# Local attention scores in 64-key by 72-query tiles: one change to a four-layer transformer kernel on one core

## The chip, the cores and the metric

The kernel runs on one core of a Trainium2 chip. The metric is the device time of one execution in microseconds (us). Before the change it is 1339.9 us (median of 4 runs, 1339.5 to 1340.6).

## The reference, cut to what matters

Two attention layers alternate with two MLP layers over x of 2048 rows by 1024 columns (bf16). In attention each of 32 heads (32 wide) looks at 8 positions, two apart, its own and 7 earlier ones:

```python
W, dil = 8, 2
off = jnp.arange(W) * dil
idx = pos[:, None] - off[None, :]                 # query s sees s, s-2, ..., s-14
...
logits = jnp.einsum("bhsd,bhswd->bhsw", q, kg) * scale
attn = _softmax(jnp.where(mask, logits, -1e9), axis=-1)
o = jnp.einsum("bhsw,bhswd->bhsd", attn, vg)
return o.transpose(...).reshape(B, S, D) @ wo
```

The kernel sorts the rows by parity, so that "two apart" becomes "next to each other": a query then sees the 8 latest rows of its own parity, a band along the diagonal.

## The kernel before

Attention goes by *units*. A unit is 4 heads of 32 (together 128 rows of q and k) of one parity, 1024 positions; there are 8 x 2 = 16 units a layer. All SBUF and PSUM tiles come from pools that hand out a fixed number of buffers in turn; a scheduler orders the instructions of each engine by when they could run, so program order is only a priority.

```python
x2p = pool("x2p", 5)     # xr, xn, xs, xo: [128, 1024] bf16
rdp = pool("rdp", 2)     # reciprocals of the softmax sums: [128, 512] f32, the same 2 KB a row
psm = pool("psm", 2, PSUM); pss = pool("pss", 2, PSUM); psa = pool("psa", 1, PSUM)   # 2, 2 and 1 buffers of 2, 4 and 4 KB a row
...
def qk_chunk(u, wts, part, n):       # 512 columns of q (part 0) or k (part 1) for unit u
    for kt in range(KD):             # 8 matmuls 128x128 by 512
        nc.tensor.matmul(ps[:], lhsT=wts[part][...], rhs=hT[:, kt, lo:lo + 512], ...)
    dst = (qT, kT)[part][g % 2]
    nc.vector.tensor_copy(out=dst[:, lo:lo + 512], in_=ps[:])

def scores(u, r):                    # r = 0, 1, 2: 3, 3 and 2 tiles of 128 keys by 136 queries
    ss = [s_tile() for _ in range(2)]
    for t in ts:
        for h in range(HG):          # 4 heads = 4 row tiles of 32
            nc.tensor.matmul(ss[h // 2][:, h % 2, ...KW], lhsT=k[hp, lo:lo + P], rhs=q[hp, lo:lo + KW], ...)
    for b in range(2):
        nc.scalar.activation(out=pv, in_=ss[b][...], func=ACT.Exp, scale=scale, bias=shift[:])
        nc.vector.tensor_tensor(out=pv, in0=pv, in1=mk, op=ALU.mult)     # 0/1 band

def values(u, b, v, oT):             # half a unit: 4 key tiles
    ...                              # v and row sums in column tiles of 32, into acc (one buffer)
    rd = rdp.tile([P, 512], FP32, name="rd", tag="rd")
    nc.scalar.activation(out=rd[:], in_=acc[:, 1, :], func=ACT.Ln)
    nc.scalar.activation(out=rd[:], in_=rd[:], func=ACT.Exp, scale=-1.0)
    nc.vector.tensor_tensor(out=oT[g][...], in0=acc[:, 0, :], in1=rd[:], op=ALU.mult)

def out_proj(c, i, oT, wo, res, dst, h2):
    xr = x2("xr"); nc.sync.dma_start(out=xr[:], in_=res(c, i))           # residual rows
    xn = x2("xn")
    ...                              # 2 x 8 matmuls, each half: xn = ps + xr on VectorE
    nc.sync.dma_start(out=rows(dst, c, i), in_=xn[:])
...
for u in range(NU):                  # fill = the 4 q/k chunks of unit u+1; in the last unit 4 out_proj
    scores(u, 0); fill[0]()
    if u: values(u - 1, 1, v, oT)
    scores(u, 1); fill[1]()
    scores(u, 2); fill[2]()
    values(u, 0, v, oT); fill[3]()
```

The softmax here doesn't subtract the row's maximum and nothing guards it: scores larger than these inputs give would overflow.

Of the kernel before, what the change touches and what calls it, by code (L numbers as in the profile page):

```python
# [9 lines left out]
ACT = mybir.ActivationFunctionType  # L10
ALU = mybir.AluOpType
FP32 = mybir.dt.float32
BF16 = mybir.dt.bfloat16

P = 128
H = 32
DH = 32
W = 8
DIL = 2
# [6 lines left out]
def kernel(  # L26
# [15 lines left out]
    nc = tc.nc  # L42
# [4 lines left out]
    KD = D // P  # L47
    FT = F // P
    NT = S // P
    SC = S // DIL  # L50
    NI = SC // P
    NG = D // P
    HG = P // DH
# [4 lines left out]
    NW2 = 4  # L58
    HF = FT // NW2
    KW = P + W  # L60
    PAD = W
    SHIFT = 14.0
    assert D == H * DH and NT == 16 and NI == 8 and NG == 8 and HG == 4
    scale = float(DH) ** -0.5

    def pool(name, bufs, **kw):
        return ctx.enter_context(tc.tile_pool(name=name, bufs=bufs, **kw))

    const = pool("const", 1)
# [2 lines left out]
    vhp = pool("vhp", NT)  # L72
    gop = pool("gop", NFB)
    wp = pool("wp", 9)
    x2p = pool("x2p", 5)
    rdp = pool("rdp", 2)
    dram = pool("dram", 1, space=bass.MemoryType.DRAM)
    psm = pool("psm", 2, space=bass.MemoryType.PSUM)
    pss = pool("pss", 2, space=bass.MemoryType.PSUM)
# [20 lines left out]
    def x2(name, shape=None, dt=BF16):  # L100
        return x2p.tile(shape or [P, D], dt, name=name, tag="x2")
# [7 lines left out]
    def ln_exp_table():  # L109
# [10 lines left out]
    nc.vector.memset(shift[:], -SHIFT)  # L120
    ones = const.tile([P, DH], BF16, name="ones")
    nc.vector.memset(ones[:], 1.0)
    band = const.tile([P, KW], BF16, name="band")
    nc.gpsimd.memset(band[:], 1.0)
    nc.gpsimd.affine_select(out=band[:], in_=band[:], compare_op=ALU.is_ge, fill=0.0, base=0,
                            pattern=[[1, KW]], channel_multiplier=-1)
    nc.gpsimd.affine_select(out=band[:], in_=band[:], compare_op=ALU.is_ge, fill=0.0, base=W - 1,
                            pattern=[[-1, KW]], channel_multiplier=1)
    b1_bf = const.tile([P, FT], BF16, name="b1_bf")
    b2_bf = const.tile([P, NI, DIL], BF16, name="b2_bf")  # L130
    b1_sb = const.tile([P, FT], FP32, name="b1_sb")
# [12 lines left out]
    Pm = [pers.tile([P, HG, NI, KW], BF16, name=f"Pm{n}") for n in range(2)]  # L144
    for t in qT:
        nc.gpsimd.memset(t[:, S:S + PAD], 0.0)

    xa = [dram.tile([S, D], BF16, name=f"xa{li}") for li in range(2)]
    xb = dram.tile([S, D], BF16, name="xb")
# [29 lines left out]
    def norm_act(dst, x, mean, rs):  # L179
        bi = st("bi", [P, 1])  # L180
        nc.vector.tensor_scalar(out=bi[:], in0=mean, scalar1=rs[:], scalar2=-1.0, op0=ALU.mult, op1=ALU.mult)
        nc.scalar.activation(out=dst, in_=x, func=ACT.Identity, bias=bi[:], scale=rs[:])

    def cols(c, i):
        return slice((c * NI + i) * P, (c * NI + i + 1) * P)
# [34 lines left out]
    def load_qk(g2):  # L220
        ts = []
        for part in range(2):
            t = wt_("wqk", [P, KD, 256])
            nc.sync.dma_start(out=t[:], in_=wq_v[:, :, part * D + g2 * 256:part * D + (g2 + 1) * 256])
            ts.append(t)
        return ts

    def qk_chunk(u, wts, part, n):
        g, c = divmod(u, DIL)
        ps = m_tile()  # L230
        lo = c * SC + n * 512
        for kt in range(KD):
            nc.tensor.matmul(ps[:], lhsT=wts[part][:, kt, (g % 2) * P:(g % 2 + 1) * P], rhs=hT[:, kt, lo:lo + 512],  # L233
                             start=(kt == 0), stop=(kt == KD - 1))
        dst = (qT, kT)[part][g % 2]
        nc.vector.tensor_copy(out=dst[:, lo:lo + 512], in_=ps[:])  # L236

    def scores(u, r):
        g, c = divmod(u, DIL)
        q, k, pm = qT[g % 2], kT[g % 2], Pm[u % 2]  # L240
        ts = range(3 * r, min(3 * r + 3, NI))
        n = len(ts)
        ss = [s_tile() for _ in range(2)]
        for t in ts:
            lo = c * SC + t * P
            for h in range(HG):
                hp = slice(h * DH, (h + 1) * DH)
                nc.tensor.matmul(ss[h // 2][:, h % 2, (t - ts[0]) * KW:(t - ts[0] + 1) * KW],  # L248
                                 lhsT=k[hp, lo:lo + P], rhs=q[hp, lo:lo + KW], start=True, stop=True)
        for b in range(2):  # L250
            pv = pm[:, 2 * b:2 * b + 2, ts[0]:ts[0] + n, :]
            nc.scalar.activation(out=pv.rearrange("p h t k -> p h (t k)"), in_=ss[b][:, :, 0:n * KW], func=ACT.Exp,  # L252
                                 scale=scale, bias=shift[:])
            mk = band[:].unsqueeze(1).unsqueeze(1).to_broadcast([P, 2, n, KW])
            nc.vector.tensor_tensor(out=pv, in0=pv, in1=mk, op=ALU.mult)  # L255

    def values(u, b, v, oT):
        g, c = divmod(u, DIL)
        pm = Pm[u % 2]
        acc = a_tile()  # L260
        hb = NI // 2
        t0 = b * hb
        for i in range(-1 if b else 0, hb):
            t = t0 + i
            for h in range(HG):
                hp = slice(h * DH, (h + 1) * DH)
                lhs = v[c][t][:, g * P + h * DH:g * P + (h + 1) * DH]
                if i < 0:
                    nc.tensor.matmul(acc[hp, 0, 0:W], lhsT=lhs, rhs=pm[:, h, t, P:KW], start=True, stop=False,
                                     skip_group_check=True)  # L270
                else:
                    w = KW if i < hb - 1 else P
                    nc.tensor.matmul(acc[hp, 0, i * P:i * P + w], lhsT=lhs, rhs=pm[:, h, t, 0:w],  # L273
                                     start=(t == 0), stop=(i == hb - 1), skip_group_check=True)
        for h in range(HG):
            hp = slice(h * DH, (h + 1) * DH)
            nc.tensor.matmul(acc[hp, 1, :].rearrange("p (t q) -> p t q", q=P), lhsT=ones[:], rhs=pm[:, h, t0:t0 + hb, 0:P],  # L277
                             start=True, stop=False, skip_group_check=True)
        s0 = t0 - 1 if b else 0
        ns = t0 + hb - 1 - s0  # L280
        o0 = (s0 + 1 - t0) * P
        for h in range(HG):
            hp = slice(h * DH, (h + 1) * DH)
            dst = acc[hp, 1, :].rearrange("p (t q) -> p t q", q=P)[:, o0 // P:o0 // P + ns, 0:W]
            nc.tensor.matmul(dst, lhsT=ones[:], rhs=pm[:, h, s0:s0 + ns, P:KW], start=False, stop=True,  # L285
                             skip_group_check=True)
        rd = rdp.tile([P, 512], FP32, name="rd", tag="rd")
        nc.scalar.activation(out=rd[:], in_=acc[:, 1, :], func=ACT.Ln)  # L288
        nc.scalar.activation(out=rd[:], in_=rd[:], func=ACT.Exp, scale=-1.0)  # L289
        lo = c * SC + t0 * P  # L290
        nc.vector.tensor_tensor(out=oT[g][:, lo:lo + hb * P], in0=acc[:, 0, :], in1=rd[:], op=ALU.mult)  # L291

    def load_wo():
        tiles = []
# [8 lines left out]
    def out_proj(c, i, oT, wo, res, dst, h2):  # L303
        xr = x2("xr")
        nc.sync.dma_start(out=xr[:], in_=res(c, i))
        xn = x2("xn")
        for n in range(NDC):
            ps = m_tile()
            xs_ = slice(n * 512, (n + 1) * 512)
            for g in range(NG):  # L310
                nc.tensor.matmul(ps[:], lhsT=oT[g][:, cols(c, i)], rhs=wo[n][g // 4][:, g % 4, :],  # L311
                                 start=(g == 0), stop=(g == NG - 1))
            nc.vector.tensor_tensor(out=xn[:, xs_], in0=ps[:], in1=xr[:, xs_], op=ALU.add)
        nc.sync.dma_start(out=rows(dst, c, i), in_=xn[:])
        h2[c][i] = vhp.tile([P, D], BF16, name="h2", tag="vh")
        mean, rs = stats(xn, 1.0 + EPS, eps2)
        norm_act(h2[c][i][:], xn[:], mean, rs)

    order = [(c, i) for c in range(DIL) for i in range(NI)]

# [70 lines left out]
    NU = NG * DIL  # L391
    for li in range(2):
# [35 lines left out]
        oT = [gop.tile([P, S], BF16, name="oT", tag="go") for _ in range(NG)]  # L428
        h2 = [[None] * NI for _ in range(DIL)]
        chunks = [(0, 0), (1, 0), (0, 1), (1, 1)]  # L430
        for part, n in chunks:
            qk_chunk(0, wts, part, n)
        wo = None
        for u in range(NU):
            last = u == NU - 1
            if not last:
                if (u + 1) % (2 * DIL) == 0:
                    wts = load_qk((u + 1) // (2 * DIL))
                fill = [lambda part=part, n=n: qk_chunk(u + 1, wts, part, n) for part, n in chunks]
            else:  # L440
                fill = [lambda i=i: out_proj(0, i, oT, wo, res, xa[li], h2) for i in range(4)]
            if u == NU - 2:
                wo = load_wo()
            scores(u, 0)
            fill[0]()
            if u:
                values(u - 1, 1, v, oT)
            scores(u, 1)
            fill[1]()
            scores(u, 2)  # L450
            fill[2]()
            values(u, 0, v, oT)
            fill[3]()
        values(NU - 1, 1, v, oT)
        for c, i in order[4:]:
            out_proj(c, i, oT, wo, res, xa[li], h2)
        g = [None] * NFB
# [38 lines left out]
```

## Time and profile before

A line of a group reads: source line, engine, operation, output<-inputs, shapes, count | busy us, mean ns of one | idle time of the engine ahead of them, and what ended it. In the chain of waits each line is start, length and what the kernel was waiting for at that time, followed back from the last instruction; "issue" is time in which an engine waited for nothing that the profile shows. PEld are TensorE's weight loads, SPq and DVEq the queues of the sync engine and of VectorE. First, from the page of the kernel before: busy times, the chain by engine, and the exponentials and masks.

```profile
PE 1312.7 (98%) x8352; PEld 590.5 (44%) x8352; DVE 428.3 (32%) x774; ACT 406.7 (30%) x622; POOL 3.9 (0%) x13
...
PE 92%; ACT 6%; DMA 1%; issue 0%; DVE 0%; SPq 0%
...
L252 ACT ACTIVATE Pm<-s,shift 128x816 bf16<-128x816 f32 (+1 forms) x192 | 152.0, 859 | 39.6 <-PE s L248 39.6
L255 DVE TENSOR_TENSOR Pm<-Pm,band 128x816 bf16<-128x816 bf16 (+1 forms) x192 | 99.9, 532 | 29.5 <-ACT Pm L252 25.0
```

TensorE (PE) bounds the kernel. Most of the rest of the chain, 6% on ScalarE (ACT), sits in the attention stages. This is the chain of waits of the kernel before over one unit:

```profile
149.11 1.83 PE m L233 x8
150.94 0.29 PE s L248 x12
151.24 1.83 PE m L233 x8
...
153.44 0.22 PE acc L277 x4
153.66 0.06 PE acc L285 x4
153.72 0.02 issue
153.74 0.61 ACT rd L288
154.35 0.02 issue
154.37 0.63 ACT rd L289
155.00 1.67 ACT Pm L252 x2
156.67 0.04 issue
156.71 0.29 PE s L248 x4
157.00 1.62 PE m L233 x7
```

A unit takes 10.09 us (149.11 to 159.20). From 153.7 to 156.7 the chain leaves TensorE: the third score block waits for a free score tile, which two exponentials hold, which stand behind Ln and Exp of the values in ScalarE's queue.

Next, busy time of the engines in stretches of the kernel before (start:end, length, then busy us and count of PE, PEld, DVE, ACT and POOL, and last the granted clock, the DMA share and GB/s): one unit; 15 units of the first layer, from its first score to its first output projection; and from there to its last output projection.

```profile
149.11:159.20 10.09, 9.79 (x117) 4.29 (x118) 6.91 (x13) 7.09 (x10) 0.00 (x0) 1.00 0.35 106
81.49:231.86 150.37, 146.22 (x1725) 64.00 (x1725) 103.07 (x180) 105.37 (x148) 0.00 (x0) 1.00 0.09 25
231.86:289.64 57.78, 57.78 (x363) 26.03 (x356) 51.26 (x102) 33.05 (x57) 0.00 (x0) 1.00 0.47 150
```

In the unit VectorE (DVE, third) is busy 6.91 and ScalarE 7.09 of 10.09 us.

### The profile page before, as it was taken

The page shows a single profiled execution, that of the slowest core. Times are in us where ns is not written, and L with a number is a line of the kernel's source. Part 1 is how long each engine was busy: PE and PEld are TensorE (multiplying, and loading weights), DVE is VectorE, ACT ScalarE, POOL GpSimd, SP SyncE. Part 2 cuts the span into 40 slices and gives each one's busy share as a digit, 9 for nine tenths or more (in the row PEclk, how much of TensorE's full clock was granted, in tenths as well). Part 3 has the DMA queues.
Part 4 walks back from the last instruction along what each step waited for, and adds up shares of the span by engine and source line. Part 5 has one row for each costly group of instructions (what it writes and reads, how often), then busy time and mean ns, then how long its engine had stood idle before and what let it go on. Part 6 is the DMA issues. An engine that isn't in the chain of part 4 may idle for free.

```text
span 1338.2 us, 19150 instructions
## 1 busy us (share of the span) xinstructions
PE 1312.7 (98%) x8352; PEld 590.5 (44%) x8352; DVE 428.3 (32%) x774; ACT 406.7 (30%) x622; POOL 3.9 (0%) x13
## 2 busy tenths in 40 slices
PE   6999999999999999999999999999999999999998
PEld 2444444444444444444444444444444444444443
DVE  6246666960000013233210667678300000011111
ACT  4346766542111110000023677675311111000000
POOL 1000000000000000000000000000000000000000
PEclk8999999999999999999999999999999999999999
DMA  9521110462222226546431101124522221334420
GB/s 251 119 64 33 33 33 28 142 194 79 63 79 77 63 71 164 129 128 181 118 95 48 34 17 33 32 74 154 151 79 79 71 81 56 119 94 124 131 89 32
DMA packets 192195, 121.83 MB, mean 91 GB/s; under 512 B 34416, under 2 KB 173680, under 8 KB 192112
## 3 DMA queue, kind: packets, MB, share of 16 engines
q1 hardware_dynamic: 192000, 120.61, 32.0%
q8 instruction: 65, 1.06, 0.3%
q0 software_dynamic: 112, 0.01, 0.1%
q14 instruction: 18, 0.15, 0.0%
HBM read 96.48 MB, written 16.78 MB: 85 GB/s over the span
## 4 chain that ended last, share of the span: by engine, by line
PE 92%; ACT 6%; DMA 1%; issue 0%; DVE 0%; SPq 0%
PE s L337 14%; PE s L380 14%; PE m L233 13%; PE m L311 8%; PE m L216 8%; PE m L380 7%; PE m L337 7%; PE acc L337 7%; PE acc L380 7%; ACT Pm L252 3%; PE s L248 1%; PE acc L273 1%; ACT rd L289 1%; ACT rd L288 1%; PE acc L277 1%; DMA x<-in_A_x_dram 1%
## 5 line engine op out<-in xcount | busy, mean ns | idle before, releaser
L380 PEld LDWEIGHTS <-w 128*128 128x128 bf16 x1792 | 175.3, 98 | 211.4
L337 PEld LDWEIGHTS <-w 128*128 128x128 bf16 x1792 | 175.3, 98 | 211.4
L233 PE MATMUL m<-hT,wqk 128*128 128x512 bf16 x1024 | 247.0, 381 | 0.0
L337 PE MATMUL s<-h,w 128*128 128x512 bf16 x896 | 202.8, 379 | 0.0
L380 PE MATMUL s<-g,w 128*128 128x512 bf16 x896 | 199.9, 379 | 0.0
L383 DVE SCALAR_TENSOR_TENSOR xo<-s,b_sb,xs 128x512 bf16<-128x512 f32 x32 | 24.0, 751 | 540.7 <-PE s L380 536.5
L252 ACT ACTIVATE Pm<-s,shift 128x816 bf16<-128x816 f32 (+1 forms) x192 | 152.0, 859 | 39.6 <-PE s L248 39.6
L233 PEld LDWEIGHTS <-wqk 128*128 128x128 bf16 x1024 | 90.3, 98 | 109.2 <-issue 6.6
L216 PE MATMUL m<-wv,hT 128*128 128x512 bf16 x512 | 113.6, 384 | 4.8 <-ACT hT L199 3.7
L311 PE MATMUL m<-wo,oT 128*128 128x512 bf16 x512 | 112.2, 379 | 0.0
L255 DVE TENSOR_TENSOR Pm<-Pm,band 128x816 bf16<-128x816 bf16 (+1 forms) x192 | 99.9, 532 | 29.5 <-ACT Pm L252 25.0
L337 PE MATMUL acc<-h,w 128*128 128x512 bf16 x448 | 103.9, 379 | 0.0
L380 PE MATMUL acc<-g,w 128*128 128x512 bf16 x448 | 100.6, 379 | 0.0
L380 PE MATMUL m<-g,w 128*128 128x512 bf16 x448 | 99.3, 379 | 0.0
L337 PE MATMUL m<-h,w 128*128 128x512 bf16 x448 | 99.0, 379 | 0.0
L163 ACT ACTIVATE ln<-mv,eps 128x1 f32<-128x1 f32 x64 | 18.7, 293 | 236.9 <-DVE mv L171 236.7
L344 ACT ACTIVATE g<-s,b_sb 128x1024 bf16<-128x1024 f32 x28 | 31.2, 1113 | 166.9 <-PE s L337 166.9
L216 PEld LDWEIGHTS <-hT 128*128 128x128 bf16 x512 | 50.3, 99 | 66.8 <-ACT hT L199 4.4
L236 DVE CAST qT<-m 128x512 bf16<-128x512 f32 x64 | 44.0, 688 | 100.3 <-PE m L233 100.1
L311 PEld LDWEIGHTS <-oT 128*128 128x128 bf16 x512 | 49.3, 98 | 59.6 <-issue 0.9
L291 DVE TENSOR_TENSOR oT<-acc,rd 128x512 bf16<-128x512 f32 x64 | 44.2, 691 | 59.0 <-ACT rd L289 58.9
L288 ACT ACTIVATE rd<-acc 128x512 f32<-128x512 f32 x64 | 38.2, 596 | 66.7 <-PE acc L285 66.7
(50 smaller groups left out, 585.6 us busy)
## 6 DMA issues: line engine op xcount, KB each, us to landing
w<-in_B_w_dram SPq DMA_DIRECT2D x56, 512.0 KB, 3.8
w<-in_B_w_dram SPq DMA_DIRECT2D x64, 448.0 KB, 4.4
wqk<-in_A_wqkv_dram SPq DMA_DIRECT2D x16, 512.0 KB, 5.1
xa<-xn SPq DMA_DIRECT2D x32, 256.0 KB, 2.1
xs<-xa SPq DMA_DIRECT2D x32, 256.0 KB, 3.1
x<-in_A_x_dram SPq DMA_DIRECT2D x16, 256.0 KB, 6.6
wv<-in_A_wqkv_dram SPq DMA_DIRECT2D x8, 512.0 KB, 5.9
xr<-in_A_x_dram SPq DMA_DIRECT2D x16, 256.0 KB, 3.0
```

The lines of the kernel that those rows point to most:

```text
L216: nc.tensor.matmul(ps[:], lhsT=hT[:, kt, cols(c, i)], rhs=wv[n][kt // 4][:, kt % 4, :], start=(kt == 0), stop=(kt == KD - 1))
L233: nc.tensor.matmul(ps[:], lhsT=wts[part][:, kt, (g % 2) * P:(g % 2 + 1) * P], rhs=hT[:, kt, lo:lo + 512], start=(kt == 0), stop=(kt == KD ...
L236: nc.vector.tensor_copy(out=dst[:, lo:lo + 512], in_=ps[:])
L252: nc.scalar.activation(out=pv.rearrange("p h t k -> p h (t k)"), in_=ss[b][:, :, 0:n * KW], func=ACT.Exp, scale=scale, bias=shift[:])
L255: nc.vector.tensor_tensor(out=pv, in0=pv, in1=mk, op=ALU.mult)
L288: nc.scalar.activation(out=rd[:], in_=acc[:, 1, :], func=ACT.Ln)
L291: nc.vector.tensor_tensor(out=oT[g][:, lo:lo + hb * P], in0=acc[:, 0, :], in1=rd[:], op=ALU.mult)
L311: nc.tensor.matmul(ps[:], lhsT=oT[g][:, cols(c, i)], rhs=wo[n][g // 4][:, g % 4, :], start=(g == 0), stop=(g == NG - 1))
L337: nc.tensor.matmul(pairs[fl][0][dc], lhsT=wt[c][:, i, fl * P:(fl + 1) * P], rhs=h2[c][i][:, dc * 512:(dc + 1) * 512], start=(k == 0), stop ...
L344: nc.scalar.activation(out=g[fb][:, fl, :].rearrange("p (n d) -> p n d", n=2), in_=t[:], func=ACT.Gelu_apprx_tanh, bias=b1_sb[:, ft:ft + 1])
L380: nc.tensor.matmul(aps[dc], lhsT=w2t[ft // HF][:, ft % HF, c::DIL], rhs=g[ft // GF][:, ft % GF, dc * 512:(dc + 1) * 512], start=(ft == 0), ...
L383: nc.vector.scalar_tensor_tensor(out=xo[:, dc * 512:(dc + 1) * 512], in0=aps[dc], scalar=b2_sb[:, i, c:c + 1], in1=xs[:, dc * 512:(dc + 1) ...
```

## The change

Per unit only an 8-wide band of each 128 x 136 score tile is used. The change computes scores in tiles of 64 keys by 72 queries, so that half a unit's scores fit in the two score tiles. A unit becomes two *visits*, each with one block of scores, one of values and two projection chunks. The exponential runs on the compact form; the mask multiply writes it into dense tiles whose other parts stay zero. With it came: k is copied out of PSUM by ScalarE, the rd tiles move into the pool of xr and xn (to make room for the compact tiles), the output weights are asked for earlier, and the TensorE order is fixed.

```diff
-    x2p = pool("x2p", 5)
-    rdp = pool("rdp", 2)
+    x2p = pool("x2p", 6)
+    pcp = pool("pcp", 2)
...
         dst = (qT, kT)[part][g % 2]
-        nc.vector.tensor_copy(out=dst[:, lo:lo + 512], in_=ps[:])
+        if part:
+            nc.scalar.copy(out=dst[:, lo:lo + 512], in_=ps[:])
+        else:
+            nc.vector.tensor_copy(out=dst[:, lo:lo + 512], in_=ps[:])
...
+        for i in range(HB):
+            for r in range(2):
+                lo = c * SC + (b * HB + i) * P + r * HK
+                for h in range(HG):
+                    mm = nc.tensor.matmul(ss[h // 2][r * HK:(r + 1) * HK, h % 2, i * HW:(i + 1) * HW],
+                                          lhsT=k[hp, lo:lo + HK], rhs=q[hp, lo:lo + HW], start=True, stop=True)
+        pc = pcp.tile([P, HG, HB, HW], BF16, name="pc", tag="pc")
+        for n in range(2):
+            nc.scalar.activation(out=pc[:, 2 * n:2 * n + 2]..., in_=ss[n][:, :, 0:HB * HW], func=ACT.Exp, ...)
+        for r in range(2):
+            nc.vector.tensor_tensor(out=pm[rp, :, b * HB:(b + 1) * HB, r * HK:r * HK + HW], in0=pc[rp], in1=mk, op=ALU.mult)
...
-        rd = rdp.tile([P, 512], FP32, name="rd", tag="rd")
+        rd = x2("rd", [P, 512], FP32)
...
+    def in_order(f, *args):
+        with tc.issue_after(last_pe[0].ins) if last_pe[0] is not None else nullcontext():
+            last_pe[0] = f(*args)
...
+        for vis in range(2 * NU):
+            u, b = divmod(vis, 2)
+            ...
+            if vis == 2 * NU - 6:
+                wo = load_wo()
+            in_order(scores, u, b)
+            if vis:
+                in_order(values, *divmod(vis - 1, 2), v, oT)
+            for n in range(2):
+                if u + 1 < NU:
+                    in_order(qk_chunk, u + 1, wts, *chunks[2 * b + n])
+                else:
+                    in_order(out_proj, 0, 2 * b + n, oT, wo, res, xa[li], h2)
```

More of the change, by code (lines that the diff above doesn't have):

```diff
@@ L60 @@
     KW = P + W
+    HK = P // 2
+    HW = HK + W
     PAD = W
@@ L122 @@
     nc.vector.memset(ones[:], 1.0)
-    band = const.tile([P, KW], BF16, name="band")
+    band = const.tile([P, HW], BF16, name="band")
     nc.gpsimd.memset(band[:], 1.0)
-    nc.gpsimd.affine_select(out=band[:], in_=band[:], compare_op=ALU.is_ge, fill=0.0, base=0,
-                            pattern=[[1, KW]], channel_multiplier=-1)
-    nc.gpsimd.affine_select(out=band[:], in_=band[:], compare_op=ALU.is_ge, fill=0.0, base=W - 1,
-                            pattern=[[-1, KW]], channel_multiplier=1)
+    for r in range(2):
+        hb_ = band[r * HK:(r + 1) * HK]
+        nc.gpsimd.affine_select(out=hb_, in_=hb_, compare_op=ALU.is_ge, fill=0.0, base=0,
+                                pattern=[[1, HW]], channel_multiplier=-1)
+        nc.gpsimd.affine_select(out=hb_, in_=hb_, compare_op=ALU.is_ge, fill=0.0, base=W - 1,
+                                pattern=[[-1, HW]], channel_multiplier=1)
     b1_bf = const.tile([P, FT], BF16, name="b1_bf")
@@ L146 @@
         nc.gpsimd.memset(t[:, S:S + PAD], 0.0)
+    for t in Pm:
+        nc.gpsimd.memset(t[0:HK, :, :, HW:KW], 0.0)
+        nc.gpsimd.memset(t[HK:P, :, :, 0:HK], 0.0)
     xa = [dram.tile([S, D], BF16, name=f"xa{li}") for li in range(2)]
@@ L232, in qk_chunk @@
         for kt in range(KD):
-            nc.tensor.matmul(ps[:], lhsT=wts[part][:, kt, (g % 2) * P:(g % 2 + 1) * P], rhs=hT[:, kt, lo:lo + 512],
-                             start=(kt == 0), stop=(kt == KD - 1))
+            mm = nc.tensor.matmul(ps[:], lhsT=wts[part][:, kt, (g % 2) * P:(g % 2 + 1) * P], rhs=hT[:, kt, lo:lo + 512],
+                                  start=(kt == 0), stop=(kt == KD - 1))
         dst = (qT, kT)[part][g % 2]
-        nc.vector.tensor_copy(out=dst[:, lo:lo + 512], in_=ps[:])
@@ L238, in scores @@
-    def scores(u, r):
+        if part:
+            nc.scalar.copy(out=dst[:, lo:lo + 512], in_=ps[:])
+        else:
+            nc.vector.tensor_copy(out=dst[:, lo:lo + 512], in_=ps[:])
+        return mm
+    last_pe = [None]
+    def in_order(f, *args):
+        with tc.issue_after(last_pe[0].ins) if last_pe[0] is not None else nullcontext():
+            last_pe[0] = f(*args)
+    HB = NI // 2
+    def scores(u, b):
         g, c = divmod(u, DIL)
         q, k, pm = qT[g % 2], kT[g % 2], Pm[u % 2]
-        ts = range(3 * r, min(3 * r + 3, NI))
-        n = len(ts)
@@ L243, in scores @@
         ss = [s_tile() for _ in range(2)]
-        for t in ts:
-            lo = c * SC + t * P
-            for h in range(HG):
-                hp = slice(h * DH, (h + 1) * DH)
-                nc.tensor.matmul(ss[h // 2][:, h % 2, (t - ts[0]) * KW:(t - ts[0] + 1) * KW],
-                                 lhsT=k[hp, lo:lo + P], rhs=q[hp, lo:lo + KW], start=True, stop=True)
-        for b in range(2):
-            pv = pm[:, 2 * b:2 * b + 2, ts[0]:ts[0] + n, :]
-            nc.scalar.activation(out=pv.rearrange("p h t k -> p h (t k)"), in_=ss[b][:, :, 0:n * KW], func=ACT.Exp,
-                                 scale=scale, bias=shift[:])
-            mk = band[:].unsqueeze(1).unsqueeze(1).to_broadcast([P, 2, n, KW])
-            nc.vector.tensor_tensor(out=pv, in0=pv, in1=mk, op=ALU.mult)
+        for i in range(HB):
+            for r in range(2):
+                lo = c * SC + (b * HB + i) * P + r * HK
+                for h in range(HG):
+                    hp = slice(h * DH, (h + 1) * DH)
+                    mm = nc.tensor.matmul(ss[h // 2][r * HK:(r + 1) * HK, h % 2, i * HW:(i + 1) * HW],
+                                          lhsT=k[hp, lo:lo + HK], rhs=q[hp, lo:lo + HW], start=True, stop=True)
@@ new lines, in scores @@
+        pc = pcp.tile([P, HG, HB, HW], BF16, name="pc", tag="pc")
+        for n in range(2):
+            nc.scalar.activation(out=pc[:, 2 * n:2 * n + 2].rearrange("p h t k -> p h (t k)"), in_=ss[n][:, :, 0:HB * HW],
+                                 func=ACT.Exp, scale=scale, bias=shift[:])
+        for r in range(2):
+            rp = slice(r * HK, (r + 1) * HK)
+            mk = band[rp].unsqueeze(1).unsqueeze(1).to_broadcast([HK, HG, HB, HW])
+            nc.vector.tensor_tensor(out=pm[rp, :, b * HB:(b + 1) * HB, r * HK:r * HK + HW], in0=pc[rp], in1=mk, op=ALU.mult)
@@ L257, in values @@
+        return mm
     def values(u, b, v, oT):
@@ L284, in values @@
             dst = acc[hp, 1, :].rearrange("p (t q) -> p t q", q=P)[:, o0 // P:o0 // P + ns, 0:W]
-            nc.tensor.matmul(dst, lhsT=ones[:], rhs=pm[:, h, s0:s0 + ns, P:KW], start=False, stop=True,
-                             skip_group_check=True)
-        rd = rdp.tile([P, 512], FP32, name="rd", tag="rd")
+            mm = nc.tensor.matmul(dst, lhsT=ones[:], rhs=pm[:, h, s0:s0 + ns, P:KW], start=False, stop=True,
+                                  skip_group_check=True)
+        rd = x2("rd", [P, 512], FP32)
         nc.scalar.activation(out=rd[:], in_=acc[:, 1, :], func=ACT.Ln)
@@ L291, in values @@
         nc.vector.tensor_tensor(out=oT[g][:, lo:lo + hb * P], in0=acc[:, 0, :], in1=rd[:], op=ALU.mult)
+        return mm
     def load_wo():
@@ L310, in out_proj @@
             for g in range(NG):
-                nc.tensor.matmul(ps[:], lhsT=oT[g][:, cols(c, i)], rhs=wo[n][g // 4][:, g % 4, :],
-                                 start=(g == 0), stop=(g == NG - 1))
+                mm = nc.tensor.matmul(ps[:], lhsT=oT[g][:, cols(c, i)], rhs=wo[n][g // 4][:, g % 4, :],
+                                      start=(g == 0), stop=(g == NG - 1))
             nc.vector.tensor_tensor(out=xn[:, xs_], in0=ps[:], in1=xr[:, xs_], op=ALU.add)
@@ L317, in out_proj @@
         norm_act(h2[c][i][:], xn[:], mean, rs)
+        return mm
     order = [(c, i) for c in range(DIL) for i in range(NI)]
@@ L430 @@
         chunks = [(0, 0), (1, 0), (0, 1), (1, 1)]
+        last_pe[0] = None
         for part, n in chunks:
-            qk_chunk(0, wts, part, n)
+            in_order(qk_chunk, 0, wts, part, n)
         wo = None
-        for u in range(NU):
-            last = u == NU - 1
-            if not last:
-                if (u + 1) % (2 * DIL) == 0:
-                    wts = load_qk((u + 1) // (2 * DIL))
-                fill = [lambda part=part, n=n: qk_chunk(u + 1, wts, part, n) for part, n in chunks]
-            else:
-                fill = [lambda i=i: out_proj(0, i, oT, wo, res, xa[li], h2) for i in range(4)]
-            if u == NU - 2:
-                wo = load_wo()
-            scores(u, 0)
-            fill[0]()
-            if u:
-                values(u - 1, 1, v, oT)
-            scores(u, 1)
-            fill[1]()
-            scores(u, 2)
-            fill[2]()
-            values(u, 0, v, oT)
-            fill[3]()
-        values(NU - 1, 1, v, oT)
+        for vis in range(2 * NU):
+            u, b = divmod(vis, 2)
+            if b == 0 and u + 1 < NU and (u + 1) % (2 * DIL) == 0:
+                wts = load_qk((u + 1) // (2 * DIL))
+            if vis == 2 * NU - 6:
+                wo = load_wo()
+            in_order(scores, u, b)
[6 more added lines that the diff above has]
+                    in_order(out_proj, 0, 2 * b + n, oT, wo, res, xa[li], h2)
+        in_order(values, NU - 1, 1, v, oT)
         for c, i in order[4:]:
```

## The prediction

> **What bounds the kernel now.** TensorE: the page has PE busy 98% of the span, and the chain that ended last is 92% PE, 6% ACT. Only the attention stages change (81.5 to 248 and 739 to 906 us). There the chain of waits repeats every 10.09 us, once per unit (16 units a layer). From single TensorE starts in the unit at 149.1 us:
> - 32 projection matmuls at 216 ns: 6.91 us.
> - Scores, 32 matmuls: four row tiles start 3 to 4 ns apart, a round of four takes 54 to 60 ns: 0.45 us.
> - Values and sums, two blocks: 1.0 us.
> - 11 changes of tile form, about 95 ns each (the next start comes 310 ns after a projection matmul instead of 216): 1.05 us. The Trainium skill, "TensorEngine Tiling (Array Packing)", Key Properties, says that changing the tiling mode drains TensorE; this trace agrees.
> - The last scores sub-block waits for a score tile, behind exponentials and Ln/Exp (the chain goes through ACT rd, rd, Pm, Pm there): its starts come 0.15 and 0.30 us late, in four half-filled rounds (0.11 more): 0.55 us.
>
> ACT is busy 7.1 and DVE 6.9 us of the 10.09 (stretch view); neither bounds, but ACT's order makes that wait.
>
> **What the change does, per unit.**
> - Scores: 64 matmuls of N=72 on 8 tiles. At the start spacing seen, eight take some 30 ns if weight loads hide: I estimate 0.15 to 0.25 us per visit, 0.4 per unit, as before.
> - Form changes: scores, values, projections, twice: 6 instead of 11. Saves 0.5 us.
> - Exponentials: 4 of 576 columns instead of 4 of 816 and 2 of 544. From 0.93 and 0.715 us I estimate 0.74 each: 3.0 instead of 5.15 us. ACT gains two k copies (0.58 each, as for v): net -1.0.
> - Masks: 4 of 1152 columns; from 0.58 and 0.435 us I estimate 0.76 each: 3.05 instead of 3.2. DVE loses two k casts (1.36): net -1.5. Both engines are off the critical path.
> - Score tiles are reused once per visit (4.5 us) and the exponentials end about 2 us into it: the 0.55 us goes. New near-collision: the last scores round of a new unit needs the second q cast, which comes behind masks and oT in DVE's queue; I allow 0.1 us.
>
> New unit: 6.91 + 0.4 + 1.0 + 0.55 + 0.1 = about 9.0 us. Saving 1.1 us on 14 middle units and 1 us together on first and last, twice: about 33 us, all on the critical path. MLP and v stages should not move.
>
> **Prediction:** 1308 us (2.4% faster), 8 in 10 between 1297 and 1325. Faster by over 2%: 0.62; within 2%: 0.36; slower: 0.02.
>
> **What would show each step.** Visit period 4.4 to 4.6 us; scores block at most 0.25 us from first to last start; three form changes per visit at 85 to 100 ns; no ACT Pm or rd in the chain of middle units; exponentials 0.70 to 0.78 us, masks 0.70 to 0.82; ACT near 6.5 and DVE near 5.8 us per unit; gemm stages unchanged.
>
> **What would make it wrong.** Weight loads of 64 columns not hiding behind 72-column matmuls, or 60 short matmuls in a row arriving too slowly: scores of 0.45 us or more per visit would halve the gain (about 1320). Masks falling out of their fast rate (over 1.1 us each) would delay the q cast and stall each new unit by up to 1 us.

## More of the kernel before

Last, from the timeline of the kernel before (start, length, engine, line, what, count, and in brackets the idle time before it): the first residual load, and the four output projections in the last unit.

```profile
46.33 1.68 SPq L305 DMA_DIRECT2D xr<-in_A_x_dram  x1
...
231.86 3.63 PE L311 MATMUL m<-wo,oT 128*128 128x512 bf16 x16
...
236.32 3.63 PE L311 MATMUL m<-wo,oT 128*128 128x512 bf16 x16
...
240.11 3.63 PE L311 MATMUL m<-wo,oT 128*128 128x512 bf16 x16
...
244.24 3.63 PE L311 MATMUL m<-wo,oT 128*128 128x512 bf16 x16
```

The residual rows of the first output projection are loaded 186 us early, and none of these projections shows a wait in brackets.

## The result, and the profile after

The changed kernel takes 1325.4 us (median of 4, 1323.7 to 1326.3), against 1339.9. The ratio is 0.989, interval 0.9873 to 0.9907. It is 14.5 us faster where 32 were forecast, and just above the range's end of 1325. The change is clear of the noise but within 2%, to which the prediction gave 0.36.

The same lines of the page of the changed kernel:

```profile
PE 1280.5 (97%) x9220; PEld 590.7 (45%) x9376; DVE 388.0 (29%) x646; ACT 372.3 (28%) x622; POOL 11.6 (1%) x19
...
PE 85%; DVE 7%; ACT 4%; DMA 2%; issue 2%; SPq 0%; DVEq 0%; ACTq 0%
...
L275 DVE TENSOR_TENSOR Pm<-pc,band 64x1152 bf16<-64x1152 bf16 x128 | 96.4, 753 | 114.1 <-ACT pc L270 112.0
...
L270 ACT ACTIVATE pc<-s,shift 128x576 bf16<-128x576 f32 x128 | 88.0, 741 | 1.2
```

The exponential (741 ns) and the mask (753 ns) came out at the forecast 0.74 and 0.76 us. But the chain is now 85% PE, and VectorE, which was 0% of it, has 7%. The chain of waits of the changed kernel over one unit:

```profile
148.43 0.46 issue
148.89 1.39 ACT pc L270 x2
...
150.30 0.76 DVE Pm L275
...
151.08 0.77 DVE Pm L275
...
151.87 0.69 DVE oT L312
152.56 0.61 DVE qT L246
153.17 0.04 issue
153.21 0.23 PE s L266 x4
...
154.20 3.42 PE m L240 x15
```

It reads: scores, exponentials, both masks, the oT multiply, the cast of q, and then the last 4 of the next 32 score matmuls. The 0.46 us of "issue" ahead of the exponentials is in part the k copy that the change gave to ScalarE: the timeline has it from 148.41 to 149.00, and the exponentials start at 148.89. From 148.43 to 153.21 TensorE's own work is not on the chain at all. It does not stand still in that time (8.87 of 9.23 us busy, below), but when it may go on with the scores is set elsewhere. The lengths by stretch, in the order used for the kernel before (one unit; first score to first output projection of layer one; from there to the last output projection):

```profile
157.53:166.76 9.23, 8.87 (x148) 4.34 (x150) 5.59 (x9) 5.99 (x10) 0.00 (x0) 1.00 0.01 3
79.65:218.57 138.92, 133.03 (x2223) 64.60 (x2252) 83.24 (x119) 90.22 (x150) 0.00 (x0) 1.00 0.10 28
218.57:281.69 63.12, 59.43 (x346) 26.52 (x345) 51.04 (x99) 30.52 (x55) 0.00 (x0) 0.97 0.43 140
```

The units gained 11.4 us in this layer, and the output projections gave back 5.3 (of which 0.9 is only moved: four of the first MLP matmuls ran inside this stretch). The granted clock of 0.97 in that stretch is not what lengthened it: in the second layer it was 1.00, and the stretch took 62.69 us. From the timeline of the changed kernel, the last unit:

```profile
218.04 0.97 SPq L327 DMA_DIRECT2D xr<-in_A_x_dram  x2
...
218.57 3.63 PE L333 MATMUL m<-wo,oT 128*128 128x512 bf16 x15
...
223.56 0.69 DVE L335 TENSOR_TENSOR xn<-m,xr 128x512 bf16<-128x512 f32 x1 [1.83 <-DMA xr<-in_A_x_dram]
...
224.31 5.30 PE L333 MATMUL m<-wo,oT 128*128 128x512 bf16 x16 [2.11 <-DVE xn L335]
...
234.91 3.61 PE L333 MATMUL m<-wo,oT 128*128 128x512 bf16 x16 [0.47 <-DVE xn L335]
```

The first residual load is issued at 218.04, half a microsecond before its projection starts, instead of 186 us ahead; xn waits for it until 223.56, and TensorE waits for xn, because both PSUM tiles of the projections are still full.

The account of the two profiled spans, in us; all terms are differences of stretch lengths. What lies ahead of the first score moved by 1.8 us; it ranged from 79.2 to 81.7 us over the profiles, the kernel before included, so it is left out of the argument.

| stretch | before | after | gain |
|---|---|---|---|
| up to the first score | 81.49 | 79.65 | 1.8 |
| units, both layers | 2 x 150.37 | 138.92 + 138.86 | 23.0 |
| first to last output projection, both | 2 x 57.78 | 63.12 + 62.69 | -10.3 |
| MLP, both (four matmuls a layer moved out of it) | 2 x 386.77 | 2 x 385.91 | 1.7 |
| the rest: v and first q and k of the second layer, the end | 66.9 | 66.8 | 0.0 |
| span | 1338.2 | 1321.9 | 16.3 |

So two things are to be explained: the units gained 23 us where the prediction has about 32, and the output projections lost some 8.5 us net where it has a small gain.

### The profile page after: what moved, and what is told of

Read it like the earlier page. It is cut to its first block, busy times and chain, and to the rows that moved or that the text cites. A ratio compares the mean times of both kernels' runs of the same rounds, so it can differ in the third digit from the quotient of the medians.

```text
span 1321.9 us, 20836 instructions
## 1 busy us (share of the span) xinstructions
PE 1280.5 (97%) x9220; PEld 590.7 (45%) x9376; DVE 388.0 (29%) x646; ACT 372.3 (28%) x622; POOL 11.6 (1%) x19
## 4 chain that ended last, share of the span: by engine, by line
PE 85%; DVE 7%; ACT 4%; DMA 2%; issue 2%; SPq 0%; DVEq 0%; ACTq 0%
PE s L403 15%; PE s L360 15%; PE m L240 10%; PE m L223 8%; PE acc L403 7%; PE m L403 7%; PE m L360 7%; PE acc L360 7%; PE m L333 7%; DVE Pm L275 3%; ACT pc L270 3%; DVE oT L312 1%; DVE qT L246 1%; DMA xr<-xb 1%; DMA xr<-in_A_x_dram 1%
## 5 line engine op out<-in xcount | busy, mean ns | idle before, releaser
L240 PE MATMUL m<-hT,wqk 128*128 128x512 bf16 x962 | 220.5, 379 | 8.2 <-issue 7.3
L240 PEld LDWEIGHTS <-wqk 128*128 128x128 bf16 x1024 | 95.3, 98 | 119.7 <-issue 12.9
L275 DVE TENSOR_TENSOR Pm<-pc,band 64x1152 bf16<-64x1152 bf16 x128 | 96.4, 753 | 114.1 <-ACT pc L270 112.0
L270 ACT ACTIVATE pc<-s,shift 128x576 bf16<-128x576 f32 x128 | 88.0, 741 | 1.2
L244 ACT CAST kT<-m 128x512 bf16<-128x512 f32 x64 | 37.5, 586 | 105.6 <-PE m L240 105.6
L225 ACT CAST v<-m 128x512 bf16<-128x512 f32 x64 | 37.4, 584 | 64.4 <-PE m L223 62.1
```

The lines of the kernel that those rows point to most:

```text
L225: nc.scalar.copy(out=v[c][i][:, n * 512:(n + 1) * 512], in_=ps[:])
L240: mm = nc.tensor.matmul(ps[:], lhsT=wts[part][:, kt, (g % 2) * P:(g % 2 + 1) * P], rhs=hT[:, kt, lo:lo + 512], start=(kt == 0), stop=(kt = ...
L244: nc.scalar.copy(out=dst[:, lo:lo + 512], in_=ps[:])
L270: nc.scalar.activation(out=pc[:, 2 * n:2 * n + 2].rearrange("p h t k -> p h (t k)"), in_=ss[n][:, :, 0:HB * HW], func=ACT.Exp, scale=scale ...
L275: nc.vector.tensor_tensor(out=pm[rp, :, b * HB:(b + 1) * HB, r * HK:r * HK + HW], in0=pc[rp], in1=mk, op=ALU.mult)
```

## The experiments

Theory A is that the q cast comes late because it stands in VectorE's in-order queue behind masks and oT. Theory B is that the residual loads come late because the rd tiles now rotate through their pool. The rivals stand in each expectation. Eleven kernels ran; all gave correct results.

### 1. q on ScalarE, k on VectorE

```diff
-        if part:
+        if not part:
             nc.scalar.copy(out=dst[:, lo:lo + 512], in_=ps[:])
```

> The changed kernel with one line turned round: ScalarE copies q out of PSUM and VectorE casts k. Theory A (the lost gain sits in VectorE's in-order queue: the q cast that the last round of scores needs stands behind two masks and the oT multiply): the score blocks' first-to-last start goes from 143 to 520 ns back to about 143 ns in every visit, visits take 4.40 us, a unit 8.80 instead of 9.23 us, twice 15 units save about 12 us: about 1313 us. Rival (the loop of scores, exponentials and masks is too long whichever engine moves q, or it is k, on ScalarE, that comes late): score blocks stay cut, 1325 us, or worse as k now waits in VectorE's queue.

Measured: 1314.4 us, ratio 0.9811 (0.9794 to 0.9827). The first-to-last start of a score block is 142 to 143 ns in all 64 visits (in the changed kernel it goes 143, 520, 263, 379 ns in turn). Visits take 4.40 and 4.43 us, a unit 8.83, and the units stretch is 132.72 us in both layers. The chain over a unit is nothing but TensorE. Theory A holds in amount: 2 x 6.2 = 12.4 us in the profile, 11 us in the medians. The output projections stretch is as long as in the changed kernel (63.9 us), so the two losses are separate. Two things move with this one line. VectorE now casts k, but early: in the trace the cast runs from 159.75 to 160.44, while VectorE would wait for the exponentials (the masks start at 161.54). And no copy stands ahead of the exponentials on ScalarE any more: with both mends (experiment 9) they start 0.35 us after the last score matmul of a block has started (164.57 after 164.21), in the changed kernel 0.45 us (148.89 after 148.44). That 0.1 us is part of the gain and was not tested alone.

### 2. The oT multiply behind the q cast, first try

```diff
-        nc.vector.tensor_tensor(out=oT[g]..., in0=acc[:, 0, :], in1=rd[:], op=ALU.mult)
+        late.append(lambda: nc.vector.tensor_tensor(out=oT[g]..., in0=acc[:, 0, :], in1=rd[:], op=ALU.mult))
...                                  # late.pop()() after the visit's first chunk
```

> The changed kernel with the oT multiply put behind the visit's first q cast in VectorE's queue; engines as in the changed kernel. Theory A: the loop of 4.82 us loses one multiply of 0.61 us and comes to 4.2 us, under the 4.40 us that TensorE needs for a visit, so score blocks run uncut and the time is about 1313 us, as when q goes to ScalarE. Rival (it matters that VectorE does the cast, or the exponentials and masks are what is late): 1325 us.

Measured: 1326.9 us, ratio 0.9901. The experiment is void: program order is only a priority, and the compiled VectorE order is the same as in the changed kernel (mask, mask, oT, q cast). It says nothing about theory A.

### 3. The same, forced

```diff
+            cast = nc.vector.tensor_copy(out=dst[:, lo:lo + 512], in_=ps[:])
+            if late:
+                with tc.issue_after(cast.ins):
+                    late.pop()()
```

> The changed kernel, VectorE still casting q, with the oT multiply really held behind the q cast in VectorE's order (the earlier try left the order as it was). Theory A as a matter of place in the queue: the loop of 4.82 us becomes 4.2 us, below a visit of 4.40, score blocks run uncut in 143 ns, about 1314 us as with q on ScalarE. Rival (it takes the other engine): score blocks stay cut, 1325 us.

Measured: 1322.9 us, ratio 0.9882 (0.9868 to 0.9895), neither 1314 nor quite 1325. In the middle units the score blocks do run uncut, in 141 to 144 ns: the place in the queue is what cut them. But a unit still takes 9.17 to 9.20 us (visits of 4.57 and 4.60 us at first, of 4.40 and 4.80 later), and the chain of this kernel shows why:

```profile
143.60 0.70 DVE oT L317
144.30 0.04 issue
144.34 0.19 PE acc L295 x4
```

The values of the next visit now wait for oT, because acc has one buffer and oT reads it. The four VectorE steps behind the exponentials add up to the same length in either order; whichever comes last holds TensorE. So theory A is to be put more widely: not the cast's place alone, but the length of the line on VectorE after the exponentials. Giving q to ScalarE works because it takes a step out of this line; the k cast that VectorE gets for it is over before the masks can start.

### 4. A longer line on purpose

```diff
             nc.vector.tensor_tensor(out=pm[rp, ...], in0=pc[rp], in1=mk, op=ALU.mult)
+            if r:
+                nc.vector.tensor_tensor(out=pm[rp, ...], in0=pc[rp], in1=mk, op=ALU.mult)
```

> The changed kernel with the second mask multiply of every visit done twice (same result, about 0.77 us more for VectorE). Theory A (a loop exponentials, masks, oT, q cast, last scores round of 4.82 us sets the pace of a unit's second visit, although VectorE is busy only some 5.8 of 9.23 us): that visit goes to about 5.6 us, and others reach the loop too, so at least 0.77 us on 30 units: 1348 us, up to 1395 us if all 62 visits run at the loop's pace. Rival (VectorE has over 3 us free in a unit and absorbs it): 1325 to 1330 us.

Measured: 1359.5 us, ratio 1.0147 (1.0133 to 1.0161): 34 us more than the changed kernel for 64 multiplies of 0.76 us, 49 us of VectorE work. The units of the first layer take 157.96 us instead of 138.92. VectorE absorbs less than a third of it, although it is idle for more than a third of the changed kernel's unit (5.59 of 9.23 us busy, above). The rival is out.

### 5. rd in a pool of its own

```diff
-    x2p = pool("x2p", 6)
+    x2p = pool("x2p", 4)
+    rdp = pool("rdp", 2)
...
-        rd = x2("rd", [P, 512], FP32)
+        rd = rdp.tile([P, 512], FP32, name="rd", tag="rd")
```

> The changed kernel with the rd tiles in a pool of their own again (2 buffers), and 4 instead of 6 buffers left for xr, xn, xs, xo: the same memory. Theory B (the reciprocal tiles rotate through the pool of the residual loads, so those loads can no longer be issued ahead of the last unit): the first residual load is issued before attention again, the wait of TensorE for xn in the last unit (about 3 us in one piece, twice) goes, the last unit takes 16 to 17 us instead of 21.6 and 21.1, and the time is about 1315 us. Rival (the fixed TensorE order, or the output weights fetched three visits earlier and the loads of the MLP weights, hold the residual loads up): 1325 us.

Measured: 1316.4 us, ratio 0.9822 (0.9808 to 0.9837). The first residual load is issued at 47.68 us again, the first-to-last projection stretches take 57.8 and 58.4 us, and the units are unchanged (138.97 and 138.89). Theory B holds.

### 6. The kernel before, with rd in the shared pool

```diff
-    x2p = pool("x2p", 5)
-    rdp = pool("rdp", 2)
+    x2p = pool("x2p", 6)
...
-        rd = rdp.tile([P, 512], FP32, name="rd", tag="rd")
+        rd = x2("rd", [P, 512], FP32)
```

> The kernel before with this one part of the change: rd tiles from the pool of xr and xn (6 buffers). Theory B: its last unit gets the wait for the residual loads too, some 4 us longer a layer: about 1348 us, the middle units stay at 10.09 us. Rival (order or weight loads of the changed kernel): 1340 us.

Measured: 1343.5 us, ratio 1.0024 (1.0009 to 1.0039). The sign is as theory B has it, and the units stay at 10.09 us, but it costs 2.3 and 1.3 us a layer instead of 4. Here the first residual load is issued at 229.97 us, 2.1 us ahead of its projection and ahead of the last MLP weight load, so it lands in time, and the wait is for a later one. Losing the early load is thus not the whole of it: where in the sync queue the load then lands decides how much it costs.

### 7. The residual loads asked for earlier, rd still in the shared pool

```diff
                 wo = load_wo()
+                for i in range(2):
+                    early.append(load_xr(0, i, res))     # out_proj takes them from there
```

> The changed kernel, rd still in the shared pool, with the first two residual loads asked for where the output weights are, five visits before the last unit. Theory B in its narrow form (what costs is that these loads stand in the sync queue behind the last MLP weight loads, which wait for the last q and k weights to be read): TensorE's 3 us wait in the last unit goes, first to last output projection falls from 63.1 to about 59 us, time about 1317 us. Rival (the shared pool itself starves the last unit of buffers): 1323 us or more.

Measured: 1317.5 us, ratio 0.9836 (0.9823 to 0.985). The two loads go out at 180.64 us, between MLP weight loads. TensorE's 2.11 us wait becomes 0.18, and the stretch falls from 63.1 and 62.7 to 60.6 and 59.5 us. What is left are waits for later loads, which stand behind the stores of earlier results in the queue (in the first layer 1.46 us for the third and fourth load and 0.92 us for the next two; in the second layer 1.06 us in one piece). So the narrow form holds for most of the loss: it is the place of the loads in the sync queue. The shared pool matters as the thing that put them there.

### 8. No fixed TensorE order

```diff
-        with tc.issue_after(last_pe[0].ins) if last_pe[0] is not None else nullcontext():
-            last_pe[0] = f(*args)
+        f(*args)
```

> The changed kernel without the fixed TensorE order. Compared as compiled, its TensorE order is the same in all middle units and differs only in the last unit of a layer, where output projections, scores and the first MLP matmuls mix otherwise. So the middle units must take 9.23 us as before; if the fixed order is what holds the last unit up, the time falls by up to 8 us to about 1317 us; if theory B is right (the residual loads come late), the last unit stays long: 1323 to 1327 us.

Measured: 1324.3 us, ratio 0.9883 (0.9869 to 0.9896), against 0.989. The units take 138.90 us, the projection stretches 60.4 and 62.7 us without any moved MLP matmuls (the changed kernel's are 62.3 and 61.8 without them). The last part of the change does next to nothing. With both mends (below), the program compiled with and without the fixed order is the same, instruction for instruction, on TensorE, VectorE, ScalarE and the sync queue, so it was not run.

### 9. Both mends

Edits 1 and 5 together.

> The changed kernel with both mends: ScalarE copies q and VectorE casts k, and rd tiles in a pool of their own (2), xr/xn/xs/xo in 4. If the two losses are separate (theories A and B, each about 10 us), they add: 1304 us, the 15 units of a layer in 132.7 us from first score to first output projection, the stretch from there to the last output projection in about 58 us. If they are one loss seen twice (a wait that only moves), about 1312 us.

Measured: 1303.6 us, ratio 0.9733 (0.9719 to 0.9746): the losses add, and this beats both kernels. Its unit, in the stretch view, the whole of the units, and the first to last projection:

```profile
164.07:172.90 8.83, 8.83 (x149) 4.13 (x148) 5.78 (x8) 5.92 (x10) 0.00 (x0) 1.00 0.01 2
80.78:213.50 132.72, 132.72 (x2254) 62.35 (x2253) 86.66 (x120) 88.21 (x149) 0.00 (x0) 1.00 0.10 29
213.50:271.44 57.94, 57.02 (x347) 25.72 (x340) 51.16 (x99) 30.52 (x55) 0.00 (x0) 1.00 0.47 150
```

And the chain of waits over one visit of it:

```profile
151.75 3.56 PE m L241 x16
155.31 0.27 PE s L267 x32
155.58 0.35 PE acc L295 x16
155.93 0.21 PE acc L299 x4
156.14 0.01 PE acc L307 x4
156.16 3.56 PE m L241 x16
```

TensorE is without a wait, as the prediction had it for the changed kernel.

### 10. Both mends, one more change of tile form a visit

```diff
-            if vis:
-                in_order(values, *divmod(vis - 1, 2), v, oT)
             for n in range(2):
+                if vis and n:
+                    in_order(values, *divmod(vis - 1, 2), v, oT)
```

> Both mends, and values put between the two projection chunks of a visit instead of behind scores: the same work, 4 instead of 3 changes of tile form a visit, 62 more in the program. If a change of form costs about 95 ns on a TensorE that waits for nothing, this is 6 us slower than both mends alone, about 1310 us, a visit about 4.50 instead of 4.41 us. If the changes overlap with something, no difference.

Measured: 1307.9 us, ratio 0.9765 (0.9752 to 0.9778). Visits take 4.51 and 4.54 us instead of 4.40 and 4.43: one change of form costs 0.107 us on a TensorE that waits for nothing, a little over the 95 ns read from starts. The whole is 4.3 us slower, not 6: over the 29 visits with values in a layer the changes are worth 3.1 us, about 6 us in all as expected, and the projection stretches gave some of it back (57.64 us instead of 57.94, although a block of values moved into them; for that reason the units stretch grew by only 2.5 us, to 135.21).

### 11. Both mends, two early residual loads

Edits 1, 5 and 7 together.

> Both mends, and the first two residual loads asked for with the output weights, so that two instead of one are issued before attention. The stretch from first to last output projection with both mends is 57.9 us, of which I estimate about 1 us to be waits left in the last unit. If these are waits for the second residual load: 56.9 us a layer and about 1302 us; if they are waits for something else, no difference from both mends: 1303.6 us.

Measured: 1303.8 us, ratio 0.973 (0.9717 to 0.9743), and a projection stretch of 57.94 us as without it. The waits left there (TensorE for xn, 1.8 us in the whole program with either kernel) are not for the second load. The trace of experiment 9 shows what they are for: the two waits of a layer (0.31 us until 217.43 and 0.61 us until 226.06) are for an xn that starts on VectorE right behind two masks and an oT multiply (216.70 and 225.32), after 2 us without a pause. It is the same line on VectorE once more.

## Why the prediction was wrong

- **TensorE's own sum was right.** New unit without the allowance: 6.91 + 0.4 + 1.0 + 0.55 = 8.86 us. Both mended kernels run units of 8.83 us. Score blocks took 143 ns from first to last start, where at most 250 were forecast. The Trainium skill, "TensorE: Matmul & The Clock Gate", Part 3, gives about 4 ns as the distance of starts on different tiles; this trace has 3 to 4 ns within a round of eight tiles of 32 x 64. The weight loads of 64 columns hid.
- **Changes of form fell from 11 to 6** at the size read from the trace: 309 instead of 216 ns into scores, and 0.107 us measured for one more (experiment 10).
- **Costs on ScalarE and VectorE were right** (0.741 and 0.753 us), and so was the removal of the old wait for score tiles.
- **The step that failed first: "Both engines are off the critical path", with the term "I allow 0.1 us" for the q cast.** It measured 0.40 us a unit: 9.23 against 8.83. The near-collision was named, but costed as one late cast; that the q cast could hold up a unit by far more was seen only for the case of slower masks, and the masks were as fast as forecast. It is a closed line: 0.46 + 1.39 us until the exponentials are done (the 0.46 with the k copy on ScalarE in it), 0.76 + 0.77 for the masks (each with its 0.02), 0.69 + 0.61 for oT and the cast, about 4.8 us from one score block to the last round of the next, while TensorE needs only 4.4. VectorE is strictly first in, first out (the Trainium skill, "TensorE: Matmul & The Clock Gate", Part 1, under "Architectural detail"); the trace agrees: in the visit at 208.07 us the cast starts at 212.42, although the last matmul of its chunk started at 210.87; the oT multiply, ahead of it in the order, started at 211.81. Over 15 units and two layers 0.40 us makes 12 us, which experiments 1 and 4 put to the test.
- **The step that failed second was missing: the rd tiles in the shared pool.** The prediction counts the line of the diff as nothing and gives the last unit a small gain; it lost about 4.3 us a layer after the moved matmuls are taken off. Experiments 5, 6 and 7 show that the residual loads lost their early place, and that their new place in the sync queue, behind MLP weight loads and result stores, sets the cost. Why the scheduler issues them in pairs in the changed kernel, and whether that makes the second wait, was not tested.
- **The two failed terms add up to the miss.** 1325.4 less 1303.6 is 21.8 us; without them the prediction would have been 4 us too high: it had allowed 0.1 us a unit for the cast and rounded the unit up to 9.0.
- "The MLP and v stages should not move" held: the MLP stretch differs by the 0.86 us of the four moved matmuls.

## What to carry to other kernels

When a change shortens the bounding engine's period, compare the new period with the length of each closed line through the other engines (from one block's result, through their in-order queues, to what the next block needs), not with their busy time: VectorE was busy 5.59 of 9.23 us and still set the pace. Changing over two copies, so that the one that is waited for left that line, was worth 11 us, where the whole change had brought 14.5. And when a diff moves a tile to another pool "for room", look up which loads rotate through that pool, and whether they still go out early.

## What the Trainium skill lacked or had wrong

- "TensorEngine Tiling (Array Packing)", Key Properties, says that changing the mode drains TensorE and gives no size. The runs show 0.093 us more into the tiled form (309 against 216 ns between starts), and 0.107 us for one more change in a visit.
- "TensorEngine Tiling (Array Packing)", Instruction Overhead, gives about 60 cycles of overhead for each matmul and warns against small free dimensions. For matmuls on different tiles that does not add up: 32 matmuls of N=72 started within 143 ns, as the start spacing in "TensorE: Matmul & The Clock Gate", Part 3, would have it. There the spacing is measured for N=512; here it holds at N=72.
- "TensorEngine Tiling (Array Packing)", Restrictions, says that column tiling disables the fast weight load. That cost nothing visible here: the 32 loads of 64 columns of a block hid in the same 143 ns.
- No page was found that says how to add up a closed line through in-order queues and compare it with the bounding engine's period; following one wait back to what ended it leads here only to the q cast. The line set the pace at moderate busy time: 0.40 us of a 9.23 us unit here, with VectorE and ScalarE at 60 to 65%.
